# Decode step on one core: the output weights wo in loads of 25, 6 and 1 rows instead of 16, 8, 4, 3 and 1

## The chip, the core and the metric

The kernel runs on one core of a Trainium2 chip. The metric is the device time in microseconds of one execution. Every time below that is not a run's time comes from one profiled execution and counts from the start of its span.

## The reference, cut to what matters

One token x of 1024 values is normalised; the result goes through an attention block (32 query heads, 4 key/value heads of 128, a window of the last 4096 positions) and beside it through a feed-forward block of 3584 hidden values. The result is the sum of x and both.

```python
def reference(A_x, A_k_cache, A_v_cache, A_wq, A_wo, B_x, B_w1, B_b1, B_w2, B_b2):
    ...
    o = jnp.einsum("bhqk,bhkd->bhqd", p, v)
    return (lambda x, *d: x.transpose(*d))(o, 0, 2, 1, 3).reshape(B, Sq, Hq * Dh) @ wo
    ...
    xn = _layernorm(x, axis=-1)
    return x + _A_ref(xn, A_k_cache, A_v_cache, A_wq, A_wo) + _B_ref(xn, B_w1, B_b1, B_w2, B_b2)
```

All data are bf16. The weights and the cache's windows are 39.9 MB; wo, of 4096 x 1024, is 8.4 MB of these and the last to be read.

## The kernel before

One program per engine, with semaphores written out by hand. SyncE (SP) issues all large loads into one queue, in the order wq, keys, w1, values, w2, wo. A load whose buffer is still read waits on SP first; wo goes into the buffers `W1` (used for w1 before) and `KT` (used for the keys before), and so waits for the matmuls of the first feed-forward layer (`C["h"]`, L422).

wo is laid out with 32 rows per partition: partition p holds rows 32p to 32p+31, and one "row" below means 128 rows of wo, one in each partition, 2 KB each. `WO_CHUNKS` gives the loads: 16 and 8 rows into `W1`, 4 and 3 into `KT`, and L427 loads the last row, 31. Each has a semaphore of its own, `s_wo[j]`.

TensorE (PE) multiplies one row c by column c of `OT`, which holds the attention's result with 32 columns. Each matmul uses 32 columns of the array, so four can stand side by side. There are two ways to add a row:

- `four_rows` takes four rows at once, one in each group of 32 columns, in two halves of 512 outputs: 4 weight loads and 8 matmuls. The four groups add into four partition groups of banks 4 and 5 (`SB`), to which the second feed-forward layer (`row_loop`) has added before. Those sums must still be added to each other: VectorE (L557) and ScalarE (L558) copy the two banks into `S`, and four f32 matmuls (L567) add the four groups of `S` into the result's four quarters.
- `fin_load` and `fin_row` take one row and add it straight to the result's quarters, which lie in bank 7 (`FB`), one quarter of 256 outputs in each group of 32 columns: 4 weight loads and 4 matmuls.

`keep_busy(n)` is a matmul of an identity in f32 with n columns, into bank 3, whose result nobody reads. `BUSY` says how many stand behind each load's rows.

The order on PE: `row_loop`; a small matmul that begins `OT` (L518); bias and x into the quarters (L544); a wait for `OT`; then for each of the loads of 16, 8 and 4 rows a wait, its groups of four, and its keep-busy matmuls. Behind the third load's groups stands the mark `C["S"]`, which releases the copies. Then comes a branch that is never taken (L559 to 562); it is tied to a hint location that was set early in the program (L320). Then the wait for both copies, the four matmuls of L567, the wait for the load of three rows and these rows one by one, the weight loads of row 31, the wait for its load, and its four matmuls (`C["fin"]`). Then ScalarE and VectorE cast the quarters to bf16 (L578, L581), and SP stores 2 KB (L583).

Weight loads and matmuls that the helpers record stand in the profile under the helpers' lines: L292 is the matmul of `go`, L494 the weight loads of `four_rows`, L531 those of `fin_load`, L298 `keep_busy`. The tile name `W<-in_A_wo_dram` is a load into `W1`.

Of the kernel before, what the change touches and what calls it, by code (L numbers as in the profile page):

```python
# [5 lines left out]
PEE = mybir.EngineType.PE  # L6
# [4 lines left out]
D = 1024  # L11
# [15 lines left out]
WQ_CHUNKS = [1, 7]  # L27
W1_CHUNKS = [8]
W2_CHUNKS = [28]
WO_CHUNKS = [16, 8, 4, 3]  # L30
WO_BULK = 28
WO_W1 = 24
DH2 = D // 2
DQ = D // 8
FB = 7
QUARTER = (0, 2, 1, 3)
SB = 4
BUSY = ((512, 384), (320, 192), (128,))


class Track:
# [11 lines left out]
def bass_parallel_sum__sliding_block_cached__mixer_channel_mlp__decode_kernel(  # L53
# [18 lines left out]
    pe, dve, act, pool, sp = nc.tensor, nc.vector, nc.scalar, nc.gpsimd, nc.sync  # L72

    def sems(name, n):
        return [nc.alloc_semaphore(f"{name}{i}") for i in range(n)]
# [5 lines left out]
    s_v = sems("s_v", 1)  # L81
    s_wo = sems("s_wo", len(WO_CHUNKS) + 1)
    s_w2 = sems("s_w2", len(W2_CHUNKS))

    PE = Track(nc, "S_PE")
# [4 lines left out]
    def sb(name, shape, d):  # L90
        return nc.alloc_sbuf_tensor(name, shape, d)
# [3 lines left out]
    W1 = sb("W1", [128, KC * F], bf16)  # L95
    KT = sb("KT", [128, HKV * W], bf16)
# [46 lines left out]
    OT = sb("OT", [128, 32], bf16)  # L143
    ZERO = sb("ZERO", [128, 1], bf16)
    S = KT[:, 2 * W:2 * W + 2 * D].bitcast(f32)
# [3 lines left out]
    def bank(b, lo=0, n=512):  # L149
        return PS[:, b * 512 + lo: b * 512 + lo + n]  # L150
# [7 lines left out]
    wo_p = A_wo.rearrange("(p j) n -> p j n", j=32)  # L158
    out_rows = out.rearrange("b s (r n) -> (b s r) n", r=2)

    C = {}


    def load_rows(dst, src, chunks, width, semaphores, first=0, c0=0, off=0):
        for j, n in enumerate(chunks):
            sp.dma_start(  # L166
                dst[:, off + c0 * width: off + (c0 + n) * width].rearrange("p (c n) -> p c n", c=n),
                src[:, first + c0: first + c0 + n, :],
            ).then_inc(semaphores[j], 16)
            c0 += n  # L170
# [111 lines left out]
    def held(out, rhs, w, pos, size, start, stop, load=False):  # L282
        return pe.add_instruction(mybir.InstMatmult(  # L283
            name=nc.get_next_instruction_name(), engine=PEE, ldweights=load,
            start_tensor_calc=start, stop_tensor_calc=stop, tile_size=size, tile_position=pos,
            ins=[pe.lower_ap(rhs), pe.lower_ap(w, for_matmul_weights=True)], outs=[pe.lower_ap(out)]))

    def low(rhs, w):
        return pe.lower_ap(rhs), pe.lower_ap(w, for_matmul_weights=True)

    def go(out, ops, pos, size, start=False, stop=False, many=False, load=True):
        return pe.add_instruction(mybir.InstMatmult(  # L292
            name=nc.get_next_instruction_name(), engine=PEE, ldweights=load,
            start_tensor_calc=start, stop_tensor_calc=stop, tile_size=size, tile_position=pos,
            ins=list(ops), outs=[pe.lower_ap(out)], bass_skip_group_check=many))

    def keep_busy(n):
        pe.matmul(bank(3, 0, n), lhsT=identf[:, :], rhs=identf[:, 0:64].unsqueeze(1).to_broadcast([128, n // 64, 64]),  # L298
                  start=True, stop=True)
# [20 lines left out]
    hinted = pe.mark_branch_hint_location()  # L320
# [18 lines left out]
    last = pe.matmul(bank(6, 16, 128), lhsT=SELQ[:, :], rhs=TQM[:, :], start=True, stop=True)  # L339
# [23 lines left out]
    for m in range(4):  # L363
        pe.wait_ge(DVE.sem, C["kt"][m])
        for c in range(4):
            w = QB[:, c * 128:(c + 1) * 128]
            pe.ldweights(w, tile_position=(0, 0))  # L367
            for nb in (2 * m, 2 * m + 1):
                last = held(bank(nb), kg[:, c, 16 * nb:16 * nb + 16, :], w, (0, 0), (128, 128), False, c == 3)
# [52 lines left out]
    C["h"] = C["lT"] = PE.mark(pe.matmul(PS[0:1, 2 * 512 + 192:2 * 512 + 320], lhsT=RS[:, 4:5], rhs=identf[:, :],  # L422
                                         is_transpose=True))
    sp.wait_ge(PE.sem, C["h"])
    load_rows(W1, wo_p, WO_CHUNKS[:2], D, s_wo[:2])
    load_rows(KT, wo_p, WO_CHUNKS[2:], D, s_wo[2:], first=WO_W1)
    sp.dma_start(KT[:, 7 * D:8 * D], wo_p[:, 31, :]).then_inc(s_wo[4], 16)  # L427

    dve.wait_ge(PE.sem, C["lT"])
    d(dve.tensor_reduce(  # L430
# [57 lines left out]
    def place(u, h):  # L488
        return PS[32 * u:32 * u + 32, (SB + h) * 512:(SB + h + 1) * 512]

    def four_rows(weights, vec, c, lo):
        w = [vec[:, c + u:c + u + 1].to_broadcast([128, 32]) for u in range(4)]
        for u in range(4):
            pe.ldweights(w[u], tile_position=(0, 32 * u))  # L494
        for h in range(2):
            for u in range(4):
                at = lo + u * D + h * DH2
                ins = go(place(u, h), low(weights[:, at:at + DH2], w[u]), (0, 32 * u), (128, 32), False, True, True, False)
        return ins
# [29 lines left out]
    def fin_load(c):  # L529
        for a in range(4):  # L530
            pe.ldweights(OT[:, c:c + 1].to_broadcast([128, 32]), tile_position=(0, 32 * a))  # L531

    def quarter(a):
        return PS[32 * a:32 * a + 32, FB * 512:FB * 512 + 2 * DQ]

    def fin_row(c):
        for a in range(4):
            lo = (c - WO_W1) * D + QUARTER[a] * 2 * DQ
            ins = go(quarter(a), low(KT[:, lo:lo + 2 * DQ], OT[:, c:c + 1].to_broadcast([128, 32])), (0, 32 * a), (128, 32),
                     False, True, True, False)  # L540
        return ins

# [1 line left out]
    pe.matmul(bank(FB, 0, 2 * DQ), lhsT=SELX[:, :], rhs=XB4[:, :],  # L544
              start=True, stop=True, skip_group_check=True)
    pe.wait_ge(DVE.sem, C["OT"])
    for j in range(len(WO_CHUNKS) - 1):
        pe.wait_ge(s_wo[j], 16)
        for c in range(sum(WO_CHUNKS[:j]), sum(WO_CHUNKS[:j + 1]), 4):
            last = four_rows(W1 if c < WO_W1 else KT, OT, c, (c if c < WO_W1 else c - WO_W1) * D)  # L550
        if j == 2:
            C["S"] = PE.mark(last)
        for n in BUSY[j]:
            keep_busy(n)
    dve.wait_ge(PE.sem, C["S"])
    act.wait_ge(PE.sem, C["S"])
    C["S0"] = d(dve.tensor_copy(S[:, 0:DH2], bank(SB)))  # L557
    C["S1"] = ACT.mark(act.activation(out=S[:, DH2:D], in_=bank(SB + 1), func=ACTF.Copy))  # L558
    nc.br("once", engines=[PEE])  # L559
    with nc.body("once", valid_engines=[PEE]):  # L560
        pe.br_lt(pe.zero_reg, 0, on_true="once", on_false="on").branch_hint(hinted)
    nc.switch_bb("on")

    pe.wait_ge(DVE.sem, C["S0"])
    pe.wait_ge(ACT.sem, C["S1"])
    for a in range(4):
        pe.matmul(quarter(a), lhsT=I32[:, 0:1].to_broadcast([128, 32]),  # L567
                  rhs=S[:, QUARTER[a] * 2 * DQ:(QUARTER[a] + 1) * 2 * DQ], start=False, stop=True, skip_group_check=True)
    pe.wait_ge(s_wo[len(WO_CHUNKS) - 1], 16)
    for c in range(WO_BULK, 31):  # L570
        fin_load(c)
        fin_row(c)
    fin_load(31)
    pe.wait_ge(s_wo[4], 16)
    C["fin"] = PE.mark(fin_row(31))

    act.wait_ge(PE.sem, C["fin"])
# [37 lines left out]
```

## Time and profile before

| | |
|---|---|
| runs (us) | 98.59, 98.64, 98.93; median 98.64 |
| the profiled execution | 98.68 us, of which the span is 97.4 |
| mean granted TensorE clock | 0.895 of full speed |
| busy | PE 53.7 us (55%), DVE 41.3 (42%), ACT 11.5 (12%), POOL 8.2 (8%) |
| read | 39.86 MB, 409 GB/s over the span |
| the chain of work that ended last | DMA 55%, DVE 22%, PE 12%, POOL 5% |
| issues of the wo loads on SP | 65.52 to 67.8 |
| `OT` ready, first matmul of a wo row | 85.94 |
| last four matmuls | 95.42 |
| cast of the result, store issued | 95.73, 96.17 |

The span is the time from the first to the last instruction; the rest of the execution's time lies around it. A share of busy time is a mean over stages with different limits. Matmuls are pipelined, and the profile models their ends, so times between starts say more than their sums. What an engine waited for is inferred from semaphores, and of several the last one is named.

### The profile page before, as it was taken

The numbers are of one execution on the slowest core, as the hardware profiler recorded it, in microseconds if no ns is written. First come the engines' busy times: TensorE is split into PE (matmuls) and PEld (weight loads), VectorE is DVE, ScalarE is ACT, GpSimd is POOL, SyncE is SP. The second block draws the span as 40 slices with busy tenths as digits, with TensorE's granted clock in tenths as the row PEclk, the third lists the DMA queues.
The fourth block names the chain that finished last, engine by engine and source line by source line (L and its number), as shares of the span: only waits on it lengthen the run. The fifth ranks groups of instructions, "written<-read, shape, count | busy, mean of one in ns | idle before, by whom it ended". The sixth has DMA issues, their size and how long they took to land.

```text
span 97.4 us, 886 instructions
## 1 busy us (share of the span) xinstructions
PE 53.7 (55%) x361; PEld 14.0 (14%) x218; DVE 41.3 (42%) x43; ACT 11.5 (12%) x22; POOL 8.2 (8%) x33
## 2 busy tenths in 40 slices
PE   0000241007933929663366189875999577877862
PEld 0000220001200002001010022112333111212320
DVE  0001221000065899999996630599941500020021
ACT  0000517000022000000000449400000000000021
POOL 6776211000000000000000000000000000000000
PEclk9999999999996555799985555999999999999999
DMA  2998888999999988889999999888899999799980
GB/s 77 707 401 377 380 377 378 401 542 431 417 431 562 448 377 377 377 377 565 404 431 431 431 569 401 377 377 377 377 542 427 431 431 431 323 431 397 422 365 11
DMA packets 1614, 39.88 MB, mean 410 GB/s; under 512 B 190, under 2 KB 204, under 8 KB 460
## 3 DMA queue, kind: packets, MB, share of 16 engines
q1 hardware_dynamic: 1588, 39.85, 95.6%
q8 instruction: 1, 0.02, 0.1%
q10 hardware_dynamic: 24, 0.01, 0.0%
q14 instruction: 1, 0.01, 0.0%
HBM read 39.86 MB, written 0.00 MB: 409 GB/s over the span
## 4 chain that ended last, share of the span: by engine, by line
DMA 55%; DVE 22%; PE 12%; POOL 5%; issue 3%; SPq 2%; ACT 1%; POOLq 0%
DMA KT<-in_A_wo_dram 29%; DMA KT<-in_A_k_cache_dram 26%; DVE KT L355 18%; PE PS L292 8%; PE PS L283 3%; DVE MX L377 2%; SPq L166 2%; POOL F L206 1%; POOL B1R L188 1%; DVE MR L388 1%; ACT Q L381 1%; POOL QB L198 1%; DVE ORow L581 0%; PE PS L385 0%; POOL I L199 0%
## 5 line engine op out<-in xcount | busy, mean ns | idle before, releaser
L355 DVE STREAM_TRANSPOSE KT<-KT 128x4096 bf16<-128x4096 bf16 x4 | 17.4, 4413 | 1.1 <-DMA KT<-in_A_k_cache_dram 1.1
L283 PE MATMUL PS<-KT,QB 128*128 128x512 bf16 x32 | 10.4, 483 | 7.6 <-DVE KT L355 7.6
L283 PE MATMUL PS<-WA,XNTb 128*32 128x512 bf16 x64 | 6.1, 553 | 7.4 <-DMA WA<-in_A_wq_dram 7.4
L292 PE MATMUL PS<-V,WA 128*128 (+1 forms) x31 | 7.9, 381 | 1.6 <-DVE LR L430 1.4
L292 PE MATMUL PS<-WA,GT 128*32 x56 | 6.7, 382 | 2.5 <-issue 1.8
L292 PE MATMUL PS<-W,YTb 128*32 x64 | 6.7, 432 | 0.8 <-issue 0.7
L253 PE MATMUL PS<-XT,onesf 128*128 128x16 f32 x2 | 0.6, 384 | 10.6 <-POOL XT L251 10.6
L327 DVE CAST Q<-PS 128x512 bf16<-128x512 f32 x1 | 0.7, 692 | 11.9 <-PE PS L283 11.9
L242 DVE STREAM_TRANSPOSE XT<-XB 128x256 bf16<-128x256 bf16 x1 | 0.6, 626 | 9.4 <-DMA XB<-in_A_x_dram 9.4
L367 PEld LDWEIGHTS <-QB 128*128 128x128 bf16 x16 | 1.8, 114 | 18.3 <-DVE KT L355 13.8
L406 DVE STREAM_TRANSPOSE WA<-WA 128x4096 bf16<-128x4096 bf16 x1 | 4.4, 4433 | 0.0
L283 PE MATMUL PS<-MRow,ML 128*128 128x512 bf16 x8 | 3.6, 626 | 0.7 <-DVE QB L348 0.7
L557 DVE COPY KT<-PS 128x512 f32<-128x512 f32 x1 | 0.7, 692 | 7.7 <-PE PS L292 7.7
L292 PEld LDWEIGHTS PS<-V,WA 128*128 (+1 forms) x32 | 3.1, 96 | 5.9 <-issue 2.9
L292 PE MATMUL PS<-W,OT 128*32 128x512 bf16 x48 | 2.9, 380 | 1.6 <-DMA W<-in_A_wo_dram 0.9
L520 DVE TENSOR_TENSOR OD<-PS,D 128x128 f32<-128x128 f32 x1 | 0.3, 292 | 8.2 <-PE PS L518 8.2
L381 ACT ACTIVATE Q<-PS 128x512 f32<-128x512 f32 x1 | 0.6, 597 | 24.0 <-DVE MX L377 24.0
L298 PE MATMUL PS<-identf 128*128 128x512 f32 (+4 forms) x10 | 3.4, 454 | 0.0
L558 ACT ACTIVATE KT<-PS 128x512 f32<-128x512 f32 x1 | 0.6, 597 | 22.4 <-PE PS L292 22.4
L402 ACT ACTIVATE WA<-PS,NMB 128x1024 bf16<-128x1024 f32 (+1 forms) x2 | 3.1, 1535 | 1.3 <-DVE NMB L397 1.3
L312 PEld LDWEIGHTS <-XNTb 128*32 128x32 bf16 x32 | 1.1, 130 | 11.8 <-DMA WA<-in_A_wq_dram 8.3
L377 DVE TENSOR_REDUCE MX<-PS 128x1 f32<-128x2048 f32 x1 | 2.3, 2291 | 0.8 <-PE PS L283 0.8
(104 smaller groups left out, 46.3 us busy)
## 6 DMA issues: line engine op xcount, KB each, us to landing
WA<-in_A_wq_dram SPq DMA_DIRECT2D x1, 7168.0 KB, 21.2
W<-in_B_w_dram SPq DMA_DIRECT2D x1, 7168.0 KB, 41.9
WA<-in_B_w_dram SPq DMA_DIRECT2D x1, 7168.0 KB, 48.2
KT<-in_A_k_cache_dram SPq DMA_DIRECT2D x1, 4096.0 KB, 25.7
V<-in_A_v_cache_dram SPq DMA_DIRECT2D x1, 4096.0 KB, 51.1
W<-in_A_wo_dram SPq DMA_DIRECT2D x1, 4096.0 KB, 20.0
W<-in_A_wo_dram SPq DMA_DIRECT2D x1, 2048.0 KB, 24.5
WA<-in_A_wq_dram SPq DMA_DIRECT2D x1, 1024.0 KB, 4.5
```

The source lines that it names most:

```text
L166: sp.dma_start(dst[:, off + c0 * width: off + (c0 + n) * width].rearrange("p (c n) -> p c n", c=n), src[:, first + c0: first + c0 + n, :], ...
L188: C["b1z"] = p(pool.memset(B1R[:, :], 0.0))
L283: return pe.add_instruction(mybir.InstMatmult(name=nc.get_next_instruction_name(), engine=PEE, ldweights=load, start_tensor_calc=start, st ...
L292: return pe.add_instruction(mybir.InstMatmult(name=nc.get_next_instruction_name(), engine=PEE, ldweights=load, start_tensor_calc=start, st ...
L298: pe.matmul(bank(3, 0, n), lhsT=identf[:, :], rhs=identf[:, 0:64].unsqueeze(1).to_broadcast([128, n // 64, 64]), start=True, stop=True)
L312: pe.ldweights(w, tile_position=(0, 32 * a))
L355: C["kt"].append(d(dve.transpose(KT[:, j * W:(j + 1) * W], KT[:, j * W:(j + 1) * W])))
L367: pe.ldweights(w, tile_position=(0, 0))
L377: C["mx1"] = d(dve.tensor_reduce(out=MX[:, 1:2], in_=PS[:, 2048:4096], axis=AX.X, op=ALU.max))
L381: C["s7"] = ACT.mark(act.activation(out=S7, in_=bank(7), func=ACTF.Copy))
L402: C[f"exp{j}"] = C["exp"] = ACT.mark(act.activation(out=PT[:, lo:lo + n], in_=src, func=ACTF.Exp, bias=NMB[:, 0:1], scale=SCALE, accum_out ...
L406: C["PT"] = d(dve.transpose(PT, PT))
```

## The change

wo comes in three loads: 25 rows into `W1`, 6 rows and then 1 row into `KT`. The keep-busy matmuls, now five of 512 columns, stand together ahead of the first load's wait. Rows 0 to 19 of the first load run in groups of four, and the mark `C["S"]` stands behind the fifth group. Rows 20 to 24 of the same load go straight to the quarters, while the copies run. The branch now stands behind the four matmuls that add `S` to the quarters. Then the six rows of the second load go straight to the quarters, and row 31 last, as before.

```diff
-WO_CHUNKS = [16, 8, 4, 3]
-WO_BULK = 28
-WO_W1 = 24
+WO_CHUNKS = [25, 6]
+WO_BULK = 25
+WO_W1 = 25
+WO_WIDE = 20
...
-BUSY = ((512, 384), (320, 192), (128,))
+BUSY = (512, 512, 512, 512, 512)
...
-    load_rows(W1, wo_p, WO_CHUNKS[:2], D, s_wo[:2])
-    load_rows(KT, wo_p, WO_CHUNKS[2:], D, s_wo[2:], first=WO_W1)
-    sp.dma_start(KT[:, 7 * D:8 * D], wo_p[:, 31, :]).then_inc(s_wo[4], 16)
+    load_rows(W1, wo_p, WO_CHUNKS[:1], D, s_wo[:1])
+    load_rows(KT, wo_p, WO_CHUNKS[1:], D, s_wo[1:], first=WO_W1)
+    sp.dma_start(KT[:, (31 - WO_W1) * D:(32 - WO_W1) * D], wo_p[:, 31, :]).then_inc(s_wo[-1], 16)
...
     def fin_row(c):
         for a in range(4):
-            lo = (c - WO_W1) * D + QUARTER[a] * 2 * DQ
-            ins = go(quarter(a), low(KT[:, lo:lo + 2 * DQ], OT[:, c:c + 1].to_broadcast([128, 32])), (0, 32 * a), (128, 32),
+            lo = (c if c < WO_W1 else c - WO_W1) * D + QUARTER[a] * 2 * DQ
+            ins = go(quarter(a), low((W1 if c < WO_W1 else KT)[:, lo:lo + 2 * DQ], OT[:, c:c + 1].to_broadcast([128, 32])), (0, 32 * a), (128, 32),
                      False, True, True, False)
         return ins
...
     pe.wait_ge(DVE.sem, C["OT"])
-    for j in range(len(WO_CHUNKS) - 1):
-        pe.wait_ge(s_wo[j], 16)
-        for c in range(sum(WO_CHUNKS[:j]), sum(WO_CHUNKS[:j + 1]), 4):
-            last = four_rows(W1 if c < WO_W1 else KT, OT, c, (c if c < WO_W1 else c - WO_W1) * D)
-        if j == 2:
-            C["S"] = PE.mark(last)
-        for n in BUSY[j]:
-            keep_busy(n)
+    for n in BUSY:
+        keep_busy(n)
+    pe.wait_ge(s_wo[0], 16)
+    for c in range(0, WO_WIDE, 4):
+        last = four_rows(W1, OT, c, c * D)
+    C["S"] = PE.mark(last)
+    for c in range(WO_WIDE, WO_BULK):
+        fin_load(c)
+        fin_row(c)
     dve.wait_ge(PE.sem, C["S"])
     act.wait_ge(PE.sem, C["S"])
     C["S0"] = d(dve.tensor_copy(S[:, 0:DH2], bank(SB)))
     C["S1"] = ACT.mark(act.activation(out=S[:, DH2:D], in_=bank(SB + 1), func=ACTF.Copy))
-    nc.br("once", engines=[PEE])
-    with nc.body("once", valid_engines=[PEE]):
-        pe.br_lt(pe.zero_reg, 0, on_true="once", on_false="on").branch_hint(hinted)
-    nc.switch_bb("on")
 
     pe.wait_ge(DVE.sem, C["S0"])
     pe.wait_ge(ACT.sem, C["S1"])
     for a in range(4):
         pe.matmul(quarter(a), lhsT=I32[:, 0:1].to_broadcast([128, 32]),
                   rhs=S[:, QUARTER[a] * 2 * DQ:(QUARTER[a] + 1) * 2 * DQ], start=False, stop=True, skip_group_check=True)
-    pe.wait_ge(s_wo[len(WO_CHUNKS) - 1], 16)
+    nc.br("once", engines=[PEE])
+    with nc.body("once", valid_engines=[PEE]):
+        pe.br_lt(pe.zero_reg, 0, on_true="once", on_false="on").branch_hint(hinted)
+    nc.switch_bb("on")
+    pe.wait_ge(s_wo[-2], 16)
     for c in range(WO_BULK, 31):
         fin_load(c)
         fin_row(c)
     fin_load(31)
-    pe.wait_ge(s_wo[4], 16)
+    pe.wait_ge(s_wo[-1], 16)
     C["fin"] = PE.mark(fin_row(31))
```

## The prediction

> **What bounds the kernel now.** I read the chain of waits first, from its end backwards.
>
> ```profile
> 67.40 27.97 DMA KT<-in_A_wo_dram
> 95.37 0.04 issue
> 95.42 0.29 PE PS L292 x4
> 95.73 0.41 DVE ORow L581
> ```
>
> The last link before the end is a transfer: the one-row load of wo, issued at 67.40, lands at 95.37. Four matmuls, a cast and the store follow, and the span ends at 97.4. So everything behind the last landing takes 2.0 us, and the diff touches none of it. A change of the time must move the start of those four matmuls, 95.42. They wait for two things: the last landing, and TensorE being through with all rows before the last.
>
> Next the transfers: the row of DMA shares, the line of SyncE's queue, and the list of DMA issues.
>
> ```profile
> DMA  2998888999999988889999999888899999799980
> q1 hardware_dynamic: 1588, 39.85, 95.6%
> W<-in_A_wo_dram SPq DMA_DIRECT2D x1, 4096.0 KB, 20.0
> W<-in_A_wo_dram SPq DMA_DIRECT2D x1, 2048.0 KB, 24.5
> KT<-in_A_wo_dram SPq DMA_DIRECT2D x1, 1024.0 KB, 26.5
> KT<-in_A_wo_dram SPq DMA_DIRECT2D x1, 768.0 KB, 27.9
> KT<-in_A_wo_dram SPq DMA_DIRECT2D x1, 256.0 KB, 28.0
> ```
>
> The queue is full from the first slices to the last loads; bytes set when wo is there. The chain gives the five issues as 65.52, 65.89, 66.38, 66.88 and 67.40, so the landings are 85.5, 90.4, 92.9, 94.8 and 95.4. The eight rows of the second load take 4.9 us, 0.61 a row. The last eight, in three loads, take from 90.38 to 95.37, 5.0 us.
>
> Last the timeline of TensorE (PE), VectorE (DVE) and ScalarE over the last ten us; columns are start, time, engine and line, and in brackets the idle time and what ended it.
>
> ```profile
> 85.94 1.90 PE L292 MATMUL PS<-W,OT 128*32 128x512 bf16 x32 [0.68 <-DVE OT L525]
> 87.77 1.77 PE L298 MATMUL PS<-identf 128*128 128x512 f32 x4
> 90.42 1.04 PE L292 MATMUL PS<-W,OT 128*32 128x512 bf16 x16 [0.88 <-DMA W<-in_A_wo_dram]
> 91.39 1.13 PE L298 MATMUL PS<-identf 128*128 128x320 f32 x4
> 92.91 0.60 PE L292 MATMUL PS<-KT,OT 128*32 128x512 bf16 x8 [0.39 <-DMA KT<-in_A_wo_dram]
> 93.44 0.49 PE L298 MATMUL PS<-identf 128*128 128x128 f32 x2
> 93.56 0.69 DVE L557 COPY KT<-PS 128x512 f32<-128x512 f32 x1 [7.68 <-PE PS L292]
> 94.30 0.64 PE L567 MATMUL PS<-KT,I 128*32 128x256 f32 x8 [0.37 <-DVE KT L557]
> 94.81 0.88 PE L292 MATMUL PS<-KT,OT 128*32 128x256 bf16 x16
> ```
>
> PE follows the landings: each piece is worked off before the next one lands, L298 fills gaps with work whose result nobody reads, and only the rows that landed last are left at the end. The three rows of the fourth load run from 94.81, right behind its landing and the sum's four quarters (L567), and are through in time for the last row.
>
> **The change, part by part, on the clock of the profiled execution.**
>
> *Fewer loads.* The same rows go through the same full queue with two issues fewer. The last eight rows in three loads took 0.1 us longer than eight rows in one, so an extra load costs 0.05 us, and two save 0.1. The landing column has one decimal, so a load may cost nothing or 0.1; the saving lies between 0 and 0.2, and I take 0.1. SP's two saved issues (0.4 to 0.5 us each) are worth nothing: they end at 67.8, and their packets wait in the queue until after 75. New landings: last row 95.27; the six rows one one-row step before (0.6), 94.65; the 25 rows at 90.38 plus one row (0.61) less one load (0.05), 90.93.
>
> By the Trainium skill, page "DMA: Bandwidth & Descriptors", section "Anatomy of one DMA — SWDGE (gpsimd) path", one DMA carries about 2.0 us of fixed cost, most of it the wait for the write's receipt; as an estimate two loads would then be worth 4.0 us and the time be 94.6. By that rule, which was fitted on another issue path, the trace disagrees: it shows 0.05 us a load, since the waits of queued loads lie on each other.
>
> *Keep-busy work.* Five matmuls of 512 columns now stand ahead of all rows, from 85.93, when OT is ready. 896 columns took 1.77 us and 512 (320 and 192) took 1.13, so 1.67 ns a column and some 0.27 at the end: 2560 columns take 4.5 us, to 90.5, half a microsecond before the 25 rows land. At the worse price of 1.77/896 a column it would be 5.1, to 91.0, and the rows would start 0.1 late. No cost taken; the wait for the load covers it.
>
> *Twenty rows four side by side.* Seven groups become five, and all come behind 90.93 + 0.04 = 90.97. Groups take 1.83 us for four (85.94 to 87.77), 0.97 for two, 0.53 for one: 0.435 each and 0.1 once. From a lone group's start to VectorE's copy is 0.65 (92.91 to 93.56), so five give 0.65 + 4 x 0.435 = 2.39, and the copy starts at 93.36 (0.2 earlier than now), ends at 94.05, and the quarters' sum starts at 94.10 (now 94.30).
>
> *Rows 20 to 24 straight to the quarters.* The price is that of the rows at the end. Windows of these lines, with PE's busy time and count for tile OT:
>
> ```profile
> 94.92:95.03 0.11, 0.11 (x8) 0.10 (x4) 0.00 (x0) 1.00 0.01 0
> ```
>
> A row's four matmuls start every 0.11 us, and the loads of their weights lie beside the row before (the x8 counts a row still in flight). Five rows: 0.55 us, from 93.24 to 93.8. They are covered by the copies, which hold PE until 94.10. Without that cover they would cost 0.55.
>
> *The sum of quarters and the branch.* L567 to the next row takes 0.51 (94.30 to 94.81), so PE is free at 94.61. The branch now stands behind it. A branch that is not taken took 0.08 us here (L561) and 0.087 at the end of the loop of L502, whose taken ones took 0.23. PE's sequencer ran it at 92.92, while the matmuls issued at 92.91 were running, so I expect it under the 0.51 us of L567: nothing. Without cover it costs 0.1 to 0.3.
>
> *Six rows, then one.* The six wait for 94.65 + 0.04 = 94.69, which is behind 94.61, so the landing decides, by only 0.08 us. Six rows take 6 x 0.11 = 0.66, to 95.35. The last row's landing allows 95.31. So PE, and no longer the load, ends last, by 0.04 us, and the last four matmuls start at 95.35 instead of 95.42.
>
> **The sum:** 0.07 us earlier. The loads' 0.1 comes in, and 0.04 is given back as the larger last piece outlasts the last landing. The profiled execution took 98.68, its span 97.4 and 1.3 around it, against a median of 98.64; so 98.61 for it and 98.57 for the median. Bounds: with loads worth 0.2 and the six rows at 0.10 each, 98.4; with loads worth nothing, rows 0.1 late at the start and 0.2 for the branch, the sum's end moves to 94.9, the last row to 95.6, and the median to 98.8. Runs of one kernel here differ by 0.34, almost all of it upwards (98.59 to 98.93), hence 98.4 to 98.95. What a measurement of this kernel can tell from no change is about 0.5%, 0.49 us: below 98.15 or above 99.13.
>
> **Rival 1, slower: an instruction fetch meets the output.** Narrowing the DMA view to the end shows this.
>
> ```profile
> q8 instruction: 1, 0.02, 5.5%
> ```
>
> That is a packet of 16 KB that starts at about 95.4, 2.5 us after the branch of L561 (92.9), and holds one DMA engine for 1.23 us (5.5% of 16 engines over 1.4 us). It starts when the wo loads are through and ends before the 2 KB store. The hint set at L320 and tied to this branch suggests that the branch releases the fetch. The new branch runs at about 94.15; a fetch 2.5 us later starts at 96.6 and ends at 97.9, where the store's packets are due at about 96.9 (issue 96.1, 97.3 landed). On the same DMA engine the store is held by about 1 us, less what had passed by then: 0.7 to 0.8 us, so 99.3. If something in PE's last instructions needs that block, the same delay falls on PE. Should the fetch instead hang on PE's position in the program, it could come earlier and meet the last loads, for up to 1.23 us, 99.8. It decides from an overlap of more than 0.5 us. Against: the store uses few engines and the fetch one. I give 22%.
>
> The Trainium skill, page "Runtime: NRT & Kernel Launch", section "Instruction fetch mechanics", says that a sequencer's instructions are refilled in 16 KiB blocks while the current one runs, and that the cost is mostly hidden. The packet's size agrees; when it is asked for is shown by no run here.
>
> **Rival 2, slower: TensorE's clock falls.** It was 0.5 from 29.7 to 40.0 and from 50.2 to 60.4, each time behind a stretch of thin work: of the 3.41 us before 50.2, PE was busy for 0.99. At half clock the five groups take 2.3 us more, L567 0.5 and the seven rows 0.8: some 102. But the new order leaves PE idle only from 90.5 to 90.97 and some tenths before 94.1, less than now (0.88 and 0.39). 4%.
>
> **Rival 3, faster: a load's fixed cost is on the path.** The smallest transfer shown, the 2 KB store, took 0.84 us from the end of its issue to the end of the wait. If two loads were each worth that, the last landing moves by 1.7 us, and PE's rows, released as early, allow about 97.0. Landings 0.6 us apart for one row speak against it. 8%.
>
> **How the numbers follow.** The forecast, 98.57, has 66%, rival 1 22%, rival 2 4%, rival 3 8%. Faster by over 0.5%: rival 3 and 1% of the forecast, 0.09. Slower by over 0.5%: rivals 1 and 2 and 3% of the forecast, 0.29. Within: 0.62. The range goes from 98.3 to 99.4: it leaves out rival 3, rival 2 and the quarter of rival 1 above 99.4, together 0.18.
>
> **What would show it.** Right: landings near 90.9, 94.65 and 95.3; the copy near 93.4; quarters' sum near 94.1; six rows behind their landing at a pace of 0.11; the last four matmuls near 95.35. Wrong: a gap between L567 and the six rows with their load already landed (the branch); the 16 KB packet under the last loads or the store, with a store that takes over 1.2 us; a granted clock under 1.0 behind 85; or last landings before 95.1.

## The result and the profile after

The changed kernel takes 101.28 us (median of 6 runs, 101.25 to 101.70), the kernel before 98.67 us on the same chips (98.55 to 99.11). The ratio is 1.026, 95% interval 1.0237 to 1.0284: slower by 2.6 us, and outside the predicted range.

The end of the chain of waits, after; columns are start, time and what ran (the diff shifts the lines: L293 is `go`, L559 VectorE's copy, L565 the sum of the quarters):

```profile
64.67 26.50 DMA W<-in_A_wo_dram
91.17 0.05 issue
91.22 2.35 PE PS L293 x40
93.60 0.70 DVE KT L559
94.35 0.64 PE PS L565 x8
94.98 0.65 PE PS L293 x17
95.64 2.19 issue
97.82 0.51 PE PS L293 x10
98.35 0.42 DVE ORow L583
```

Before, the last transfer in the chain was that of the last row. Now it is that of the 25 rows, and behind it stands work of TensorE (PE), apart from VectorE's copy, broken by 2.19 us of "issue": time in which PE waited for nothing that the profile knows. The timeline shows where in the rows it falls.

```profile
91.22 2.88 PE L293 MATMUL PS<-W,OT 128*32 128x512 bf16 x60 [0.56 <-DMA W<-in_A_wo_dram]
94.35 0.64 PE L565 MATMUL PS<-KT,I 128*32 128x256 f32 x8 [0.25 <-DVE KT L559]
94.92 0.72 PE L293 MATMUL PS<-KT,OT 128*32 128x256 bf16 x18
97.82 0.49 PE L293 MATMUL PS<-KT,OT 128*32 128x256 bf16 x10 [2.19 <-issue]
97.83 0.20 PEld L532 LDWEIGHTS <-OT 128*32 128x32 bf16 x8 [2.47 <-issue]
```

The last seven rows are 28 matmuls. 18 of them run at the expected pace: four rows and half of the fifth. A gap in the middle of a row is odd, since a row's four matmuls wait for nothing between them. No load is missing either. The six rows were issued at 65.05 and the last row at 65.52; with the times to landing in the list of issues they landed at about 94.9 and 95.5.

```profile
KT<-in_A_wo_dram SPq DMA_DIRECT2D x1, 1536.0 KB, 29.8
KT<-in_A_wo_dram SPq DMA_DIRECT2D x1, 256.0 KB, 30.0
```

Behind the gap come 10 matmuls and 8 weight loads: the last 18 instructions of PE's program. The DMA view of 95.3 to 96.7 us holds just two packets, both instructions; each column of its first two lines is a slice of 0.035 us.

```profile
DMA  0060900000000000000000000000000000000000
GB/s 0 0 234 0 468 0 0 0 0 0 0 0 0 0 0 0 0 0 0 0 0 0 0 0 0 0 0 0 0 0 0 0 0 0 0 0 0 0 0 0
q8 instruction: 1, 0.02, 4.1%
q14 instruction: 1, 0.01, 1.5%
```

The 16 KB packet starts at 95.46 and takes 0.92 us (4.1% of 16 engines over 1.4 us); PE goes on 2.36 us after its start. A packet of the same size came at 95.4 in the kernel before, where nobody waited for it.

The gap accounts for most of the loss. From the first of the seven rows to the cast it is 3.43 us here and 0.98 in a run without the gap (456 instructions, below): 2.19 for the gap and some 0.26 more that the rows take when broken in two. The rest of the 2.6 us, some 0.17, lies ahead of it: the last row landed 0.12 later in this profile than in that of the kernel before, and the larger last piece outlasts the landing.

### The profile page after: what moved, and what is told of

It reads as the page before. It is cut to its first block, busy times and chain, and to the rows that moved or that the text cites. A ratio compares the mean times of both kernels' runs of the same rounds, so it can differ in the third digit from the quotient of the medians.

```text
span 100.0 us, 924 instructions
## 1 busy us (share of the span) xinstructions
PE 54.5 (54%) x378; PEld 14.8 (15%) x242; DVE 41.2 (41%) x43; ACT 11.5 (12%) x22; POOL 8.2 (8%) x33
## 4 chain that ended last, share of the span: by engine, by line
DMA 52%; DVE 24%; PE 12%; POOL 5%; issue 4%; ACT 1%; POOLq 0%
DMA W<-in_A_wo_dram 27%; DMA KT<-in_A_k_cache_dram 26%; DVE KT L356 17%; PE PS L293 11%; DVE MX L376 2%; DVE MX L378 2%; POOL F L207 1%; POOL B1R L189 1%; DVE KT L559 1%; DVE MR L389 1%; PE PS L565 1%; ACT Q L382 1%; POOL QB L199 1%; DVE ORow L583 0%; PE PS L386 0%
## 5 line engine op out<-in xcount | busy, mean ns | idle before, releaser
L284 PE MATMUL PS<-KT,QB 128*128 128x512 bf16 x32 | 9.2, 438 | 7.6 <-DVE KT L356 7.6
L284 PE MATMUL PS<-WA,XNTb 128*32 128x512 bf16 x64 | 6.8, 600 | 7.4 <-DMA WA<-in_A_wq_dram 7.4
L293 PE MATMUL PS<-V,WA 128*128 (+1 forms) x32 | 8.2, 381 | 1.4 <-DVE WA L407 1.1
L293 PE MATMUL PS<-WA,GT 128*32 x56 | 6.7, 382 | 3.4 <-issue 1.8
L293 PE MATMUL PS<-W,YTb 128*32 x64 | 6.8, 487 | 0.5 <-issue 0.3
L299 PE MATMUL PS<-identf 128*128 128x512 f32 x10 | 4.6, 602 | 0.7 <-DVE OT L526 0.7
L293 PEld LDWEIGHTS PS<-V,WA 128*128 (+1 forms) x32 | 3.1, 96 | 6.0 <-issue 3.0
L559 DVE COPY KT<-PS 128x512 f32<-128x512 f32 x1 | 0.7, 692 | 7.5 <-PE PS L293 7.5
L293 PE MATMUL PS<-W,OT 128*32 128x512 bf16 (+1 forms) x60 | 2.9, 344 | 0.6 <-DMA W<-in_A_wo_dram 0.6
L293 PEld LDWEIGHTS PS<-WA,GT 128*32 x28 | 1.4, 92 | 8.8 <-issue 8.8
```

Of the source, the lines that this page charges most:

```text
L284: return pe.add_instruction(mybir.InstMatmult(name=nc.get_next_instruction_name(), engine=PEE, ldweights=load, start_tensor_calc=start, st ...
L293: return pe.add_instruction(mybir.InstMatmult(name=nc.get_next_instruction_name(), engine=PEE, ldweights=load, start_tensor_calc=start, st ...
```

## The experiments

The suspicion from the profile: the instructions themselves are late. The change makes PE's program, as it is compiled, longer. A group of four rows is 12 instructions (4 weight loads, 8 matmuls), a single row 8. Before: 7 groups and 4 single rows, 84 + 32 = 116. After: 5 groups and 12 single rows, 60 + 96 = 156. With one separate wait less it grows by 39, from 438 instructions to 477 (each loop's body counted once), and 477 - 18 = 459 stand ahead of the gap.

**The threshold, in the kernel before.** Weight loads that nothing uses stand in PE's idle time around 15 us, where PE waits for wq; the cut shows 21 of them, the other run has 22:

```diff
+            if j == 1:
+                for _ in range(21):
+                    pe.ldweights(vec[:, 0:1].to_broadcast([128, 32]), tile_position=(0, 0))
             pe.wait_ge(semaphores[j], 16)
```

With 21, 459 instructions:

> The kernel before with 21 weight loads more that nothing uses, set into TensorE's idle time around 15 us: its program grows from 438 to 459 instructions. Theory A (length): the last instruction is just the last of the block; no change, 98.5 to 99.1. Rivals B and C: no change either. With the next run it gives the threshold.

With 22, 460 instructions:

> The kernel before with 22 such weight loads, one more than in the run with 21: 460 instructions. Theory A (length): the very last matmul lies in the next block; a gap of 2.0 to 2.6 us stands between the last row's third and fourth matmul, about 101.2 us, though no part of the change is in it. Rivals B and C: no change, 98.5 to 99.1.

Measured: 99.24 and 100.99 us. The timelines, first with 21, then with 22:

```profile
94.91 0.89 PE L292 MATMUL PS<-KT,OT 128*32 128x256 bf16 x16
```

```profile
94.81 0.87 PE L292 MATMUL PS<-KT,OT 128*32 128x256 bf16 x15
97.64 0.37 PE L292 MATMUL PS<-KT,OT 128*32 128x256 bf16 x1 [1.96 <-issue]
```

One weight load, 80 us earlier, splits off exactly the last matmul and puts 1.96 us in front of it. No part of the change is in this kernel. The reading is that the 460th instruction lies in the next block, which is fetched late. The time with 22 is 0.2 below its forecast, since the gap is 1.96 and not 2.0 to 2.6. The run with 21 is at 99.24, above its forecast: its span, 97.5, is near the 97.4 of the kernel before, and the rest came outside the span (below).

**The branch back in its old place**, all else as changed:

```diff
     C["S1"] = ACT.mark(act.activation(out=S[:, DH2:D], in_=bank(SB + 1), func=ACTF.Copy))
+    nc.br("once", engines=[PEE])
...
-    nc.br("once", engines=[PEE])
```

> The changed kernel with the never-taken branch back behind the copies, in front of the four matmuls of the quarters' sum; nothing else differs, and TensorE's program stays 477 instructions long. Theory A (length): TensorE's program is fetched in blocks, and its 459th instruction is the last of the block that is there in time; the last 18 wait for a fetch that only starts when TensorE gets near them. The branch's place is of no matter: about 101.3 us, 18 matmuls of the last seven rows, a gap of 2.2 us with no releaser, then 10. Rival B (place): the branch starts the fetch (in the changed kernel the 8 KB packet follows it by 1.0 us); run some 0.6 to 0.8 us earlier it starts the fetch as much earlier, the gap shrinks to 1.4 to 1.6 us: 100.5 to 100.7.

Measured: 101.25 us. The branch ran at 92.6 instead of 94.4, and still:

```profile
94.74 0.72 PE L293 MATMUL PS<-KT,OT 128*32 128x256 bf16 x18
97.47 0.80 PE L293 MATMUL PS<-KT,OT 128*32 128x256 bf16 x10 [2.01 <-issue]
```

The same 18 and 10. The 16 KB packet came at 95.1 instead of 95.46, the gap ended 0.35 us earlier. So moving the branch by 1.8 us shifted the packet by 0.36 and the gap's end as much, and left the time as it was; the break's place is set by length.

**The branch alone, in the kernel before**, moved behind the four matmuls of L567:

```diff
-    nc.br("once", engines=[PEE])
...
+    nc.br("once", engines=[PEE])
...
     pe.wait_ge(s_wo[len(WO_CHUNKS) - 1], 16)
```

> The kernel before with the branch alone moved behind the four matmuls of the quarters' sum, as the change does; 438 instructions. Theories A and E: the packets come 1.0 us after the branch, at about 95.3 as before, and nothing of the program waits for them: no change, 98.5 to 99.1. Rival B (the late branch itself costs the 2.6 us): about 101.

Measured: 98.83 us in one run, beside a median of 98.84 for the kernel before: this part of the change alone costs nothing that shows.

**The change with a shorter program.** The tail is untouched; the loop of the first feed-forward layer, 30 us ahead of it, does one step per turn, and one keep-busy matmul falls away: 456 instructions.

```diff
-    with pe.Fori(0, KC // 2) as i:
-        for u in range(2):
+    with pe.Fori(0, KC) as i:
+        for u in range(1):
...
-BUSY = (512, 512, 512, 512, 512)
+BUSY = (512, 512, 512, 512)
```

> The changed kernel with TensorE's program shortened early on and the tail untouched: the loop of the first feed-forward layer has one step per turn instead of two (17 instructions fewer, four taken branches more, some 30 us before the end), and four keep-busy matmuls stand in place of five (4 fewer): 456 instructions. Theory A (length): all of it lies within 459, no gap, the last four matmuls follow the last landing or the six rows; 98.5 to 98.9 us. Rival B (place of the branch) and rival C (the wait for larger loads): the gap of 2.2 us stays, about 101.3.

Measured: 99.04 us, just above its forecast; the ratio to the kernel before is 1.0026 (1.0001 to 1.0052). The gap is gone:

```profile
94.20 0.64 PE L565 MATMUL PS<-KT,I 128*32 128x256 f32 x8 [0.24 <-DVE KT L559]
94.78 0.94 PE L293 MATMUL PS<-KT,OT 128*32 128x256 bf16 x28
95.76 0.42 DVE L583 CAST ORow<-PS 64x256 bf16<-64x256 f32 x1 [1.61 <-PE PS L293]
```

All 28 matmuls in one run. The span is 97.4, as before, but the profiled execution took 99.05, so 1.65 us lay outside the span; with 459 instructions it was 99.24 - 97.5 = 1.74, against 98.68 - 97.4 = 1.3 in the kernel before and 1.3 in the changed one. If the end of the program waits for the same block, a few more spare instructions should take it away. With the loop of the first feed-forward layer as in the last run, the attention's second product unrolled by three instead of five, and three keep-busy matmuls in a loop, the program has 443:

```diff
-PV_UNROLL = 5
+PV_UNROLL = 3
...
-    with pe.Fori(0, KC // 2) as i:
-        for u in range(2):
+    with pe.Fori(0, KC) as i:
+        for u in range(1):
...
-    for n in BUSY:
-        keep_busy(n)
+    with pe.Fori(0, 3) as i:
+        keep_busy(512)
```

> The changed kernel with a shorter program for TensorE: one step per turn in the loop of the first feed-forward layer, three in place of five in the attention's second product, and three keep-busy matmuls in a loop in place of five written out: 443 instructions, 16 under 459 (the run with 456 had 3 to spare and the kernel before has 21). Loads, rows and the order of the tail are those of the change. Theory A: no gap; span 97.3 to 97.5. In the run with 456 instructions the execution was 1.65 us longer than its span, against 1.3 in the kernel before; if that is the program's end waiting for the same block, it is 1.3 to 1.45 here, and the time is 98.6 to 98.9, the same as before within 0.3%. If the span's surroundings have another cause (the loads, the semaphores), 99.0 to 99.1 as with 456.

Measured: 98.87 us, ratio 1.0007 (0.9981 to 1.0034); span 97.6, execution 98.88, 1.3 outside. Both halves fit: no gap, and the time outside the span is back to 1.3.

**What keeps the block away.** PE's program sets a hint at its start, tied to the never-taken branch. Both taken out, so that these runs don't tell the two apart:

```diff
-    hinted = pe.mark_branch_hint_location()
...
-    nc.br("once", engines=[PEE])
-    with nc.body("once", valid_engines=[PEE]):
-        pe.br_lt(pe.zero_reg, 0, on_true="once", on_false="on").branch_hint(hinted)
-    nc.switch_bb("on")
```

From the changed kernel:

> The changed kernel without the never-taken branch and without the hint at the start of TensorE's program: 472 instructions, 13 over 459. Theory H (the hint holds the next block back until its branch has run): without it the block is asked for earlier, packets well before 94 us, no gap; 98.7 to 100.0, the packets' time under the loads included. Theory P (position alone): packets at about 95.3 as before, a gap of 2.0 to 2.2 us behind 20 of the last 28 matmuls; about 101.2.

From the kernel before:

> The kernel before without the branch and the hint: 433 instructions. Theory H: the two packets come in the middle of the loads and hold a DMA engine for about 1 us each; no gap, 98.7 to 99.9. Theory P: packets at about 95.3, no change, 98.5 to 99.2.

Measured: 100.01 and 100.18 us, no gap in either; the second is above its forecast. The changed kernel's program is 472 instructions long here, so 13 lie behind the 459th. The DMA view of 64.5 to 66 us in the second one, where the kernels with the hint have no instruction packet:

```profile
DMA  0999900999990000000000000000000090000000
q1 hardware_dynamic: 16, 0.92, 144.0%
q8 instruction: 1, 0.02, 3.9%
```

The block comes at 64.8 (64.7 in the first), in the middle of the loads, and holds one DMA engine for 0.95 us. The landing ahead of it, of the values, is where it was (58.9 against 58.8 in the kernel before); the next one, of w2, comes at 77.3 instead of 75.8. That is paid at the end: the chain of the kernel before without the hint has its last landing at 96.87 instead of 95.37.

```profile
67.15 29.73 DMA KT<-in_A_wo_dram
96.87 0.04 issue
96.92 0.29 PE PS L292 x4
```

So in these two programs the hint with its branch keeps the fetch out of the loads, which is worth about 1.5 us to the kernel before (100.18 against 98.62 beside it, one run each), and the price is that the block is not there at the end. Without it the same edit costs nothing that shows in one run each (100.01 against 100.18); with it, 2.6 us.

**Longer still.** The edit of the first two runs, with `range(150)`, in the changed kernel: 627 instructions.

> The changed kernel with 150 unused weight loads more in TensorE's idle time around 15 us: 627 instructions, so that the 459th falls among the first matmuls behind the wait for the 25 rows, and the place near it where the block was asked for so far (within the 36 instructions ahead of it) among the keep-busy matmuls or just ahead of them, at 85 to 90 us. Theory A (the block is asked for by position, and takes some 2.8 us from there): the 8 and 16 KB packets come at 85.5 to 90.5, the block is there when the rows land, no gap although the program is longer than ever; the packets hold a DMA engine each for about 1 us under the loads of wo, so the last landing comes 0 to 1.2 later: 98.7 to 100.0. Theory A2 (the block is asked for only at the end of the program or by the copies): packets again at about 95.3 and a gap at the first group of rows, from 91.2 to about 97.8, 104 or more. Rival D (the time grows with the number of instructions): over 101.3.

Measured: 100.00 us, no gap. The forecast time held, the place of the packet did not: it came at 26.8 us, not at 85 to 90, although this kernel has the hint; a second one came at 96.7, 1.2 us behind the branch, and nothing waited for it. The loads behind the first were late all the same: wq had landed at 22.3 as in the other runs, the keys landed at 33.6 instead of 32.0 to 32.2, and the 25 rows at 92.35 instead of 91.17. The longest program of all is 1.3 us faster than the changed kernel, so the time doesn't grow with the length; what costs the 2.19 us is the step into a block that has not come.

**The branch further ahead**, between the twenty and the five rows:

```diff
     C["S"] = PE.mark(last)
+    nc.br("once", engines=[PEE])
...
     for c in range(WO_WIDE, WO_BULK):
...
-    nc.br("once", engines=[PEE])
```

> The changed kernel with the never-taken branch between the twenty and the five rows of the first load, 40 instructions ahead of the copies' wait; 477 instructions. So far the packets came 1.01 to 1.02 us after the branch where TensorE could go on behind it at once (the changed kernel, and the runs with 456 and 627 instructions), and some 1.0 us after the end of the copies' wait where the branch stood right in front of that wait. Theory E (the branch, and TensorE's next step behind it, release the fetch): here nothing holds TensorE behind the branch, which runs at about 92.6; packets at 93.6, the gap ends some 2.4 us after them, at 96.0 to 96.3, but the packets come under the last loads and hold one engine back for about 1 us: the end is set by the one or the other, 99.5 to 100.2. Theory P (position alone): packets at about 95.2 as in the changed kernel and gap as there, 101.2.

Measured: 100.33 us, 0.13 above its forecast.

```profile
95.22 0.72 PE L293 MATMUL PS<-KT,OT 128*32 128x256 bf16 x18
96.85 0.49 PE L293 MATMUL PS<-KT,OT 128*32 128x256 bf16 x10 [0.92 <-issue]
```

The gap shrank to 0.92, because the 16 KB packet came at 94.49, before the copies were done and ahead of L569 (the sum of quarters, 94.68). So the packet does not hang on the copies' end or the last rows, which come later; it comes behind the branch. But my lag of 1.0 us was wrong here: the branch ran at 91.7, the packet came 2.8 us behind it. Over the runs with the hint the last 16 KB packet comes 2.3 to 2.8 us behind the branch where that runs at 91.7 to 93.0, under the loads, and 1.1 to 1.2 behind it where it runs at 94.2 or later, as the loads end. That a full queue stretches the fetch is argued from these numbers and not tried by itself.

## Why the prediction was wrong

**What failed.** Every part was costed by the time of its instructions, and none by their number. The step on rows 20 to 24 and the one on the last seven rows (0.11 us a row) have the right pace, but 12 single rows instead of 4 make the program 39 instructions longer, and the 460th and later were not there. The sum has no term for the wait for them, which measured 2.19 us. Before, 21 instructions were spare; 0.07 us of forecast gain stood against this cliff.

**Rival 1 had the packet and the wrong victim.** The 16 KB packet of the before profile was read, its tie to the branch suspected, and its price worked out for the store, 0.7 to 0.8 us. One sentence said that PE's last instructions might need the block, and priced it the same. That term was mis-sized. In the four runs with a gap the packet starts at 95.46, 95.10, 95.26 and 94.49, and PE goes on 2.36, 2.37, 2.38 and 2.36 us later, so the gap's end moves with the packet; the packet itself is 0.9 to 1.1 of that. The packet's time was off as well: 2.5 us behind the branch were forecast, and in the changed kernel it came 1.1 behind it. The store took 1.2 us from its issue to the end of the span in all runs compared. In the changed kernel without the hint a second 16 KB packet starts at 98.18, beside the store issued at 97.51, and the 1.2 us stay.

The Trainium skill, page "Runtime: NRT & Kernel Launch", section "Instruction fetch mechanics", says that instructions come in 16 KiB blocks of 256 and that crossing a boundary is mostly hidden. The packet's size agrees, and in the changed kernel without the hint, which runs 13 instructions past the border, no gap showed. With the hint the step was not hidden: the gap was 1.96 to 2.19 us in three runs and 0.92 in the fourth.

**Fewer loads.** Forecast 0.1 us (between 0 and 0.2); the runs show none. In the changed kernel's profile the three landings came at 91.17, 94.87 and 95.50, each 0.2 us behind the forecast. The last landings in four profiles with five loads are 95.37, 95.48, 95.37 and 95.53, in four with three loads (the changed kernel, the branch put back, 456 and 443 instructions) 95.50, 95.33, 95.36 and 95.52: 95.44 against 95.43. The profiles with a packet earlier than 95 are left out. Within each four the values differ by 0.16 and 0.19, so a saving of up to 0.1 can't be ruled out. The 0.1 us came from two rows of one profile. Rival 3, at 1.7 us for two loads, is out.

**What held.** Keep-busy work ended ahead of the 25 rows. From their first matmul to the copy took 2.38 (forecast 2.39), the copy took 0.70, the sum followed 0.05 behind it and the first of the six rows 0.57 behind the sum's start (0.69, 0.05, 0.59): the rows waited for their landing, as forecast, and started 0.05 behind it. The 0.51 us that the prediction took for the sum is an upper bound, since in the kernel before, too, the next row started 0.05 behind its landing at 94.76; in that kernel without the hint the same stretch is 0.46. The branch behind the sum cost nothing. With 456 instructions the seven rows follow each other at 0.11, and the cast starts 0.40 behind the last landing instead of 0.36: the 0.04 us by which PE was to end last. TensorE's granted clock in the changed kernel was 1.00 in all stretches from 91.2 to 98.4, so rival 2 is out. Without the gap, then, the change makes no difference that shows (1.0007 with 443 instructions, 0.9981 to 1.0034), as was forecast; whether the 0.07 us of gain are there, these runs can't tell.

## What to carry to other kernels

Cost an edit in instructions as well as in time: count them per engine, and look in the profile for instruction packets and where they fall. Here the mark of a missing instruction block was a gap put down to "issue", in the middle of work that needs nothing new, with all loads landed and a 16 KB instruction packet shortly before its end. It is settled cheaply: add idle instructions far ahead of the suspected place, one by one, and see whether the break moves.

## What the runs showed of the hardware

- With the hint and its branch, TensorE's program here runs to its 459th instruction without waiting for a fetch; in the programs of 460 and 477 the 460th waits for a 16 KB packet that comes behind the branch. One instruction makes the difference: 99.24 and 100.99 us, one run each.
- A 16 KB instruction packet under a full load queue took 0.92 to 0.95 us of one DMA engine, and the last landing came 1.2 to 1.5 us later, with the packet at 27 us (one run) and at 65 (two). Why it is more than the packet's own time is not shown.
- A program that ends just under the border pays outside the span: 1.65 and 1.74 us around it with 456 and 459 instructions, 1.3 with 438 and 443, and 1.3 with 460 and more. That the runtime's own instructions behind the program wait for the block is the likely reason; no row shows them.
- Open: why the border lies behind the 459th instruction; which position of PE asks for the block when no hint holds it back (64.7 us in one program); why the hint did not hold the first block back in the program of 627 instructions (26.8 us); and what the 8 KB packet on q14 is, which in the run with the branch furthest ahead came at 90.0, before the branch.
